# Block-sparse attention and a SwiGLU layer: scoring eight gathered key blocks per query block in place of all keys under a mask

## The chip, the cores and the metric

The kernel runs on one NeuronCore of a Trainium2 chip. Its five engines take their instructions in order, each from its own stream, and meet through semaphores: TensorE (PE; its weight loads are listed as PEld) multiplies matrices into PSUM, VectorE (DVE) and ScalarE (ACT) work elementwise, GpSimd (POOL) does small work and issues DMAs, SyncE (SP) issues DMAs. The metric is the device time of one execution in microseconds; lower is better.

## What is computed

Attention over 4 batches, 8 heads, 768 positions of 64 elements, followed by a gated layer over the 3072 tokens of 512 elements. Positions come in 24 blocks of 32. A query block attends its own block and the two neighbours, the first and the last block, and three blocks drawn for it in `sampled_blocks`; the first and the last query block attend everything.

```python
mask = np.abs(blk_i - blk_j) <= window
mask = mask | (blk_i == 0) | (blk_j == 0) | (blk_i == n_blocks - 1) | (blk_j == n_blocks - 1)
for qb in range(n_blocks):
    for kb in sampled_blocks[qb]:
        mask[qb * block:(qb + 1) * block, kb * block:(kb + 1) * block] = True
scores = np.where(mask, scores, -1000000000.0)
attn = softmax(scores);  out = attn @ v
...
xn = x / rms * rms_g
out = (silu(xn @ w_gate) * (xn @ w_val)) @ w_out      # 512 -> 1536 -> 512
```

## The kernel before

**Tiling.** Tokens go in groups: three of 256 tokens for batch 0, then two of 384 for each other batch. Within a group the heads follow one another. For one head, `scores` (L321 to L335) multiplies all 768 keys, six tiles of 128 on the output's partitions, with the group's queries as columns (L330), and one exponential on ScalarE takes 768 columns out of PSUM (L333). `values` (L337 to L343) multiplies each 128x128 piece of the exponentials, as the stationary operand, with the head's 64 value columns and two columns of ones (66 columns, L341); the ones column gives the sum, whose reciprocal (L350) scales the output into `stage` (L351).

**The mask** is part of the product: `KT` and `QT` carry, below their 64 rows of data, 24 rows that hold the key's block and the query's mask (88 rows in all). What is not attended is computed and comes out of the exponential as zero.

**The gated layer.** For a finished group, squares are summed on VectorE (L375), POOL takes the power -0.5 (L383), and x is scaled and turned, either by TensorE (L424, L428) or by a DMA transpose from SP (L395, L400). The FFN is cut into pieces (`ffn_pieces`): `gate(f)` (four matmuls, L442, then tanh on ScalarE, L446), `val(f)` (four matmuls, L453, then two VectorE instructions, L457 and L459) and `down` (L470, three matmuls a piece; the last one is copied out by ScalarE, L476, and stored by SP). Pieces share three PSUM buffers.

**What sets the order.** Every stream is written out by hand. The pieces of one group's FFN are spread at an even rate over the next group's heads: `position()` is called between the parts of the scores and emits what is due. The value products of a head come one head late (`late_pv`), and a group's FFN is entered two heads into the next group (`TX = 2`). The first group runs by itself (`first_group`), with matmuls on zeros (`keep_busy`) in TensorE's gaps. The last group's FFN forms the tail.

**Loads.** POOL loads K and Q with a cast to bf16 (L89, L81), V in float32 (L101) and the weights (L111, L553). VectorE casts V (L120). Batch 0's K and Q are turned by TensorE (L287) and copied by VectorE (L292). For later batches SP issues DMA transposes (L300) and further DMAs that put the halves in place (L308).

Of the kernel before, what the change touches and what calls it, by code (L numbers as in the profile page):

```python
# [11 lines left out]
I32 = mybir.dt.int32  # L12
# [6 lines left out]
def kernel(  # L19
# [20 lines left out]
    NB = S // 32  # L40
    NC = S // P
    DM = H * D
    DFF = moe_w_gate.shape[1]
    KD = DM // P
    MASKV = -65536.0
    SCALE = 1.0 / (D ** 0.5)
    NRND = sampled_blocks.shape[1]
    NF = DFF // P
    HC = NC // 2
    TGM = HC * P  # L50

    groups = [(0, c, 2) for c in range(0, NC, 2)]
    groups += [(b, c, HC) for b in range(1, B) for c in range(0, NC, HC)]
    FIRST = NC // 2
    KR = D + NB
    NP = H // 2
    VW = D + 2
    VS = D + 16
# [6 lines left out]
    work = ctx.enter_context(tc.tile_pool(name="work", bufs=1))  # L65
    ps_f = ctx.enter_context(tc.tile_pool(name="ps_f", bufs=3, space=bass.MemoryType.PSUM))
# [3 lines left out]


    qbf, kbf, vraw, qrest = {}, {}, {}, {}

    def load_q0(pr, lo, hi):

        if lo == 0:
            t = qbf[(0, pr)] = ld.tile([P, 2, 2 * D], BF16, name="q0", tag="q0", bufs=3)
        else:
            t = ld.tile([P, 2, NC * D], BF16, name="qbf", tag="qbf", bufs=4)[:, :, lo * D:]
            qrest[(0, pr)] = t  # L80
        nc.gpsimd.dma_start(  # L81
            out=t, in_=q[0, 2 * pr:2 * pr + 2].rearrange(
                "e (p c) d -> p e (c d)", p=P)[:, :, lo * D:hi * D])

    def load_one(b, pr, store, t=None):
        src, name = (k, "kbf") if store is kbf else (q, "qbf")
        if t is None:
            t = ld.tile([P, 2, NC * D], BF16, name=name, tag=name, bufs=4)
        nc.gpsimd.dma_start(  # L89
            out=t,  # L90
            in_=src[b, 2 * pr:2 * pr + 2].rearrange("e (p c) d -> p e (c d)", p=P))
        store[(b, pr)] = t

    def load_qk(b, pr):
        load_one(b, pr, kbf)
        load_one(b, pr, qbf)

    def load_v(b, pr):
        t = ld.tile([P, 2, NC, D], FP32, name="vraw", tag="vraw" if b else "vraw0",
                    bufs=2 if b else 4)  # L100
        nc.gpsimd.dma_start(  # L101
            out=t, in_=v[b, 2 * pr:2 * pr + 2].rearrange("e (p c) d -> p e c d", p=P))
        vraw[(b, pr)] = t
# [81 lines left out]
    for pr in range(1, NP):  # L185
        load_one(0, pr, kbf)
        load_q0(pr, 0, 2)
        if pr > 1:
            load_v(0, pr - 2)
# [641 lines left out]
```

## Time and profile before

| | |
|---|---|
| median of 3 runs | 309.54 us (309.23 to 316.04) |
| profiled execution | 309.93 us, its span 308.2 us |
| first FFN matmul | 26.23 us after the span's start |
| exponentials on ScalarE | 192, 813 ns each (768 columns) |
| score matmuls | 432: 288 of 384 columns, 144 of 256 |
| value matmuls | 1152 of 66 columns (a few are missing from the trace) |
| gate and value matmuls of the FFN | 432 each: 288 of 384 columns, 144 of 256 |
| POOL busy | 54.7 us, mostly the issue of DMAs at about 720 ns |
| DMA engines, share of the first 15 of 40 slices | 0.7 to 0.9 and over |

Lines of the profile read as: line of the kernel, engine, operation, output and inputs by the program's names with partitions x elements and type, count; busy time and mean of one in ns; idle time of the engine just ahead of it and what ended that. A matmul's duration holds its latency, so a run of matmuls takes less than the sum of its durations; the pace is read from runs of different lengths. Busy time of POOL counts the issue of its DMAs.

### The profile page before, as it was taken

The numbers are of one execution on the slowest core, as the hardware profiler recorded it, in microseconds if no ns is written. First come the engines' busy times: TensorE is split into PE (matmuls) and PEld (weight loads), VectorE is DVE, ScalarE is ACT, GpSimd is POOL, SyncE is SP. The second block draws the span as 40 slices with busy tenths as digits, with TensorE's granted clock in tenths as the row PEclk, the third lists the DMA queues.
The fourth block names the chain that finished last, engine by engine and source line by source line (L and its number), as shares of the span: only waits on it lengthen the run. The fifth ranks groups of instructions, "written<-read, shape, count | busy, mean of one in ns | idle before, by whom it ended". The sixth has DMA issues, their size and how long they took to land.

```text
span 308.2 us, 7249 instructions
## 1 busy us (share of the span) xinstructions
PE 299.9 (97%) x2843; PEld 198.9 (65%) x2863; DVE 203.6 (66%) x561; ACT 204.8 (66%) x330; POOL 54.7 (18%) x81
## 2 busy tenths in 40 slices
PE   8889999999999999999999999999999999999995
PEld 6676886985787566656666566655666566655653
DVE  7788884885578567763768457682767546675860
ACT  4886775776888677757776676676767667732331
POOL 9846201042220212012200122010000100010000
PEclk9999999999999999999999999999999999999999
DMA  7999999999999478526673379614000130002002
GB/s 124 276 210 201 208 215 151 171 173 245 218 205 146 112 154 162 109 48 189 113 156 85 81 176 148 140 25 139 16 2 0 42 115 2 0 5 100 2 0 103
DMA packets 61082, 36.71 MB, mean 119 GB/s; under 512 B 38348, under 2 KB 56640, under 8 KB 61048
## 3 DMA queue, kind: packets, MB, share of 16 engines
q0 software_dynamic: 17120, 17.90, 32.7%
q1 hardware_dynamic: 43892, 18.35, 27.5%
q8 instruction: 22, 0.36, 0.5%
q14 instruction: 12, 0.10, 0.1%
q10 hardware_dynamic: 36, 0.01, 0.0%
HBM read 28.59 MB, written 6.29 MB: 113 GB/s over the span
## 4 chain that ended last, share of the span: by engine, by line
PE 91%; POOL 3%; DMA 3%; DVE 2%; issue 1%; ACT 0%; POOLq 0%
PE gp L442 21%; PE vp L453 20%; PE yp L470 20%; PE st L330 18%; PE op L341 11%; DMA qbf<-in_q_dram 3%; POOL kbf L89 1%; PE tx L424 1%; POOL vraw L101 1%; POOL q L81 1%; DVE junk L375 1%; DVE stage L368 0%; PE tqk L287 0%; DVE xs L403 0%; POOL ki_i L183 0%
## 5 line engine op out<-in xcount | busy, mean ns | idle before, releaser
L333 ACT ACTIVATE ex<-st 128x768 bf16<-128x768 f32 x186 | 150.0, 813 | 53.7 <-PE st L330 51.9
L330 PE MATMUL st<-QT,KT 88*128 88x384 bf16 (+1 forms) x432 | 93.9, 309 | 1.4 <-DVE QT L292 1.0
L442 PE MATMUL gp<-xg,wg 128*128 128x384 bf16 (+1 forms) x432 | 80.8, 307 | 0.0
L453 PE MATMUL vp<-xg,wv 128*128 128x384 bf16 (+1 forms) x432 | 80.2, 307 | 0.0
L457 DVE SCALAR_TENSOR_TENSOR u<-th,gp 128x384 bf16<-128x384 bf16 (+1 forms) x108 | 54.8, 508 | 38.1 <-ACT th L446 36.6
L470 PE MATMUL yp<-wo,hps 128*128 128x512 bf16 (+1 forms) x283 | 71.9, 369 | 0.9
L446 ACT ACTIVATE th<-gp 128x384 bf16<-128x384 f32 (+1 forms) x108 | 49.1, 454 | 27.8 <-PE gp L442 27.5
L459 DVE TENSOR_TENSOR hps<-u,vp 128x384 bf16<-128x384 bf16 (+1 forms) x108 | 55.1, 510 | 11.3
L330 PEld LDWEIGHTS <-KT 88*128 88x128 bf16 x432 | 41.5, 98 | 26.1 <-DVE QT L292 2.0
L453 PEld LDWEIGHTS <-wv 128*128 128x128 bf16 x432 | 40.6, 97 | 20.6 <-issue 0.2
L442 PEld LDWEIGHTS <-wg 128*128 128x128 bf16 x432 | 40.1, 97 | 20.5 <-issue 0.3
L341 PEld LDWEIGHTS <-ex 128*128 128x128 bf16 x1116 | 42.8, 97 | 8.4 <-issue 0.2
L341 PE MATMUL op<-Vp,ex 128*128 128x66 bf16 x1116 | 44.9, 193 | 0.0
L470 PEld LDWEIGHTS <-hps 128*128 128x128 bf16 x300 | 27.6, 97 | 22.6 <-DMA wo<-in_moe_w_out_dram 0.3
L383 POOL TENSOR_TENSOR rstd<-ssq,mhalf 128x3 f32<-128x3 f32 (+1 forms) x9 | 7.4, 817 | 143.1 <-DVE ssq L375 143.1
L350 DVE RECIPROCAL rz<-op 128x3 f32<-128x3 f32 (+1 forms) x64 | 11.2, 174 | 24.0 <-PE op L341 23.7
L476 ACT ACTIVATE yo<-yp 128x512 f32<-128x512 f32 (+1 forms) x25 | 14.4, 577 | 15.4 <-PE yp L470 15.4
L351 DVE TENSOR_TENSOR stage<-op,rz 128x192 bf16<-128x192 f32 (+1 forms) x64 | 21.8, 341 | 2.2
L101 POOL DMA_DIRECT2D vraw<-in_v_dram x16 | 11.8, 739 | 59.3 <-DVE Vp L120 55.7
L375 DVE CUSTOM_DVE_ANT_0 junk<-stage 128x448 bf16<-128x448 bf16 (+1 forms) x24 | 14.7, 611 | 0.5
L395 DVE SCALAR_TENSOR_TENSOR xs<-stage,rstd,gain 128x512 bf16<-128x512 bf16 x15 | 10.4, 746 | 4.4 <-POOL rstd L383 4.4
L89 POOL DMA_DIRECT2D qbf<-in_q_dram x12 | 8.6, 721 | 16.8 <-DMA turned<-qbf 15.4
(71 smaller groups left out, 112.2 us busy)
## 6 DMA issues: line engine op xcount, KB each, us to landing
vraw<-in_v_dram POOLq DMA_DIRECT2D x16, 384.0 KB, 5.2
out_dram<-yo SPq DMA_DIRECT2D x23, 256.0 KB, 2.3
kbf<-in_k_dram POOLq DMA_DIRECT2D x15, 192.0 KB, 6.0
qbf<-in_q_dram POOLq DMA_DIRECT2D x12, 192.0 KB, 6.3
KT<-turned SPq DMA_DIRECT2D x24, 96.0 KB, 3.7
QT<-turned SPq DMA_DIRECT2D x22, 96.0 KB, 2.9
wg<-in_moe_w_gate_dram POOLq DMA_DIRECT2D x4, 384.0 KB, 10.7
wv<-in_moe_w_val_dram POOLq DMA_DIRECT2D x4, 384.0 KB, 12.1
```

Of the source, the lines that this page charges most:

```text
L101: nc.gpsimd.dma_start(out=t, in_=v[b, 2 * pr:2 * pr + 2].rearrange("e (p c) d -> p e c d", p=P))
L330: nc.tensor.matmul(out=at[:, e, 0:tg], lhsT=KT[b % 2][0:KR, h, jt * P:(jt + 1) * P], rhs=QT[b % 2][0:KR, h, c0 * P:c0 * P + tg], start=Tru ...
L333: nc.scalar.activation(out=ex[:, nj * part:nj * (part + 1), :], in_=at[:, 0:nj, 0:tg], func=AF.Exp, scale=SCALE)
L341: nc.tensor.matmul(out=op[:, it, 0:VW], lhsT=ex[:, jt, it * P:(it + 1) * P], rhs=Vp[b % 2][:, h, 2 * (jt % HC) + jt // HC, 0:VW], start=(j ...
L351: nc.vector.tensor_tensor(out=stage[:, 0:n, h * D:(h + 1) * D], in0=op[:, 0:n, 0:D], in1=rz[:, 0:n].unsqueeze(2).to_broadcast([P, n, D]), ...
L375: nc.vector.tensor_tensor_reduce(out=junk[:, 0:hi - lo], in0=part, in1=part, scale=1.0, scalar=(e["ssq"][:, it:it + 1] if lo else DM * 1e- ...
L442: nc.tensor.matmul(out=gp[:, 0:tg], lhsT=wg[:, c, f * P:(f + 1) * P], rhs=xg[:, c, 0:tg], start=(c == 0), stop=(c == KD - 1))
L446: nc.scalar.activation(out=th[:, 0:tg], in_=gp[:, 0:tg], func=AF.Tanh, scale=0.5)
L453: nc.tensor.matmul(out=vp[:, 0:tg], lhsT=wv[:, c, f * P:(f + 1) * P], rhs=xg[:, c, 0:tg], start=(c == 0), stop=(c == KD - 1))
L457: nc.vector.scalar_tensor_tensor(out=u[:, 0:tg], in0=th[:, 0:tg], scalar=1.0, in1=gp[:, 0:tg], op0=ALU.add, op1=ALU.mult)
L459: nc.vector.tensor_tensor(out=hps[:, f, 0:tg], in0=u[:, 0:tg], in1=vp[:, 0:tg], op=ALU.mult)
L470: nc.tensor.matmul(out=yp, lhsT=hps[:, f, tt * P:(tt + 1) * P], rhs=wo[:, f, lo:hi], start=(f == 0), stop=(f == NF - 1))
```

## The change

The whole attention part is rewritten. Work goes in 24 chunks of 128 queries (four query blocks of 32), six per batch: five with consecutive inner blocks, and one "edge" chunk with blocks 0, 23, 1 and 22. The edge chunk is the last of its batch, in the last batch the last but one. FFN groups are of 2, 2, 4, 4, 4, 4 and 4 chunks.

For each inner query block eight key blocks, 256 keys, are gathered: a window of three (three slots), three sampled ones and the two outer ones. `KT` and `QN` keep a head's even positions on 64 partitions and the odd ones on the other 64, so 256 keys are 128 columns of `kg`; the queries are laid out block-diagonally in `Qd`. One matmul of 64 columns per head and query block gives all its scores. Blocks 0 and 23 of the edge chunk are scored against all of `KT`. An exponential now takes 1024 columns.

Which sampled block a slot takes is computed on the chip at the start: 39 small VectorE instructions make a table of row indices `vidx`, and registers (44 on ScalarE, 22 on POOL) are loaded with offsets into `KT`. The window and outer keys are copied by VectorE, the sampled ones by ScalarE (two of three) and POOL, at addresses from the registers. Values are cast into `Vs` (batch 0 by ScalarE and VectorE, later ones by POOL) and written by SP to a DRAM table, one row of 2112 bytes for two positions and all heads. POOL gathers 128 rows of it per query block by an indirect DMA, 88 in all. Where a sampled block repeats one that is already there, its index points to rows of zeros, ones column included.

A value matmul has 32 columns of weights (one query block) and writes 32 partitions of PSUM, the four query blocks of a chunk in turn, so that the array is used in column tiles.

```diff
+    sizes = [2, 2, 4, 4, 4, 4, 4]
...
+    vtab = [dram.tile([NT + HB, 2 * HV], BF16, name=f"vtab{i}") for i in range(B)]
...
+    for eng, of in ((ET.Activation, range(NRND - 1)), (ET.Pool, range(NRND - 1, NRND))):
+        for r in of:
+            _, vals = nc.values_load_multi_w_load_instructions(
+                kofs[0:1, r * NB + 1:(r + 1) * NB - 1], engines=[eng], min_val=0, max_val=NT - HB,
...
+    def table(b):
+        nc.sync.dma_start(out=vtab[b][0:NT, :].rearrange("(p c) x -> p (c x)", c=HC),
+                          in_=Vs[b % 2].rearrange("p c h x -> p (c h x)"))
+
+    def turn(b, pr, which, copy, spare=False):
+        src = raw.pop((b, pr, which))
+        p_, tag = (ps_f, "ff") if spare else (ps_o, "ot")
+        t = p_.tile([P, 2, HC, P], BF16, name="tqk", tag=tag)
+        for e in range(2):
+            for cc in range(HC):
+                nc.tensor.transpose(out=t[:, e, cc, :], in_=src[:, e, cc * P:(cc + 1) * P],
+                                    identity=ident)
...
+    def gather_k(i, copy):
+        b, qbs = chunks[i]
+        kg = kgs[i] = work.tile([P, H, QB, P], BF16, name="kg", tag="kg", bufs=2)
...
+        copy(out=kg[:, :, j0:j0 + n, 0:WIN],
+             in_=spaced(src[:, :, (qbs[j0] - 1) * HB:(qbs[j0] - 1) * HB + WIN], step, n, WIN))
+        for w, at in ((0, 0), (1, NT - HB)):
+            copy(out=kg[:, :, j0:j0 + n, G0 + w * HB:G0 + (w + 1) * HB],
+                 in_=src[:, :, at:at + HB].unsqueeze(2).to_broadcast([P, H, n, HB]))
+
+    def sampled_k(i):
...
+            copy = act if r + 1 < NRND else pool
+            copy(out=kgs[i][:, :, j, R0 + r * HB:R0 + (r + 1) * HB],
+                in_=KT[b % 2][:, :, bass.ds(kat[(qbs[j], r)], HB)])
...
+    def gather_q(i, copy):
...
+            for a in range(2):
+                for w in range(2):
+                    src = QN[b % 2][w * D:(w + 1) * D, :, qbs[lo] * HB:(qbs[lo] + 1) * HB]
+                    copy(out=dst[a * D:(a + 1) * D, :, lo:hi, a, w, :],
+                         in_=spaced(src, step, hi - lo, HB))
+
+    def gather_v(i):
+        b, qbs = chunks[i]
+        vg = vgs[i] = work.tile([P, QB, 2 * HV], BF16, name="vg", tag="vg", bufs=2)
+        for j in range(QB):
+            if qbs[j] not in (0, NB - 1):
+                nc.gpsimd.indirect_dma_start(
+                    vg[:, j, :], None, vtab[b][:],
+                    bass.IndirectOffsetOnAxis(ap=vidx[:, qbs[j]:qbs[j] + 1], axis=0))
...
+            for j in range(2 if wide else 0, QB):
+                nc.tensor.matmul(out=st[:, at:at + UN], lhsT=kgs[i][:, h, j, :],
+                                 rhs=Qd[i % 2][:, h, j, :], start=True, stop=True)
...
+        def mm(hh, j, lhsT, rhs, n, of):
+            nc.tensor.matmul(out=op[j * BLK:(j + 1) * BLK, hh, :], lhsT=lhsT, rhs=rhs,
+                             start=(n == 0), stop=(n == of - 1))
...
+        if not in_order(i):
+            nc.vector.scalar_tensor_tensor(
+                out=xs, in0=stages[i], scalar=rstds[i], in1=gain, op0=ALU.mult, op1=ALU.mult)
+            nc.sync.dma_start_transpose(out=xg[:, :, at:at + P], in_=xs)
+            return
...
+    for i in range(len(chunks)):
...
+        scores(i, 0)
+        loads(i)
+        at(0)
+        if i > 0:
+            x_turned(i - 1)
+            if group_of[i - 1] != group_of[i]:
+                enter(group_of[i - 1], NPOS * len(groups[group_of[i]])
+                      + (4 if group_of[i] == len(groups) - 1 else 0))
+        scores(i, 1)
+        at(1)
...
+        if nx is not None and not newbatch and i > 0:
+            gather_v(nx)
+        at(2)
...
+        if nx is not None and not newbatch and i > 0:
+            gather_k(nx, dve)
+            gather_q(nx, dve)
+            dyn += sampled_k(nx)
+        at(3)
+        values(i, 0)
+        at(4)
+        at(5)
+        values(i, 1)
+        squares(i)
+        rms_power(i)
+        at(6)
+        at(7)
+        if nx is not None and (newbatch or i == 0):
+            if i == 0:
+                for pr in range(NP):
+                    turn(0, pr, 1, (act, dve)[pr % 2], spare=pr % 2)
+            gather_k(nx, dve)
+            gather_q(nx, dve)
+            for x in sampled_k(nx):
+                x()
+            gather_v(nx)
```

`at(n)` emits a chunk's side jobs (casts, turns and the table of the next batch), its share of the sampled copies for the next chunk, and the FFN pieces that are due; `NPOS` is 8 positions per chunk. `loads(i)` issues the next batch's V from SP and its K and Q from POOL. Tokens of chunks 0 to 3 and of the last group are turned by TensorE (four transposes and four scaled copies per chunk), the others by DMA transpose; stores go by query block, for the latter as two half-blocks each.

## The prediction

> **What bounds the kernel now.** I read the busy table first, then the chain that ended last, then the stretches by stage, and last single instructions in order of time.
>
> ```profile
> PE 299.9 (97%) x2843; PEld 198.9 (65%) x2863; DVE 203.6 (66%) x561; ACT 204.8 (66%) x330; POOL 54.7 (18%) x81
> ...
> PE 91%; POOL 3%; DMA 3%; DVE 2%; issue 1%; ACT 0%; POOLq 0%
> PE gp L442 21%; PE vp L453 20%; PE yp L470 20%; PE st L330 18%; PE op L341 11%; DMA qbf<-in_q_dram 3%; POOL kbf L89 1%; PE tx L424 1%; POOL vraw L101 1%; POOL q L81 1%; DVE junk L375 1%; DVE stage L368 0%; PE tqk L287 0%; DVE xs L403 0%; POOL ki_i L183 0%
> ```
>
> TensorE is busy for 97% of the span and carries 91% of the chain. The three FFN products are 61% of it, the scores 18%, the value products 11%. VectorE and ScalarE idle a third of the time, so a saving on them is worth nothing here; one on TensorE is worth its own length.
>
> The start matters too. In the next answer each line gives start, duration, engine, line and operation; the first is the first FFN matmul, the others give the pace of small value matmuls.
>
> ```profile
> 26.23 1.04 PE L442 MATMUL gp<-xg,wg 128*128 128x256 bf16 x4
> ...
> 14.43 0.89 PE L341 MATMUL op<-Vp,ex 128*128 128x66 bf16 x24
> 18.15 0.53 PE L341 MATMUL op<-Vp,ex 128*128 128x66 bf16 x12
> ```
>
> The FFN begins at 26.2 us; from there TensorE never rests. Twelve more value matmuls take 0.36 us more, so one with 66 columns costs 0.0303 us. In the same way (longer run minus single, or the chain's 4.53 us for 21) I get 0.058 us at 128 columns, 0.109 at 256, 0.1625 at 384, 0.216 at 512. With these paces the 282 us behind 26.2 come out as FFN 187 + scores 57 + values 32 + transposes 3 = 279, so the paces can be trusted.
>
> **The change, on TensorE after the FFN begins.** The FFN keeps its columns: 192 gate and value matmuls at 0.109, 480 at 0.216, 288 down matmuls at 0.216: 187 us. Scores: an ordinary chunk has 32 matmuls of 64 columns, about 0.0295 each (the 66-column row scaled): 0.94 us; an edge chunk 24 of 128 and 16 of 64: 1.86 us. Two chunks run before the FFN, so 18 x 0.94 + 4 x 1.86 = 24.5 us, against 57. Here the change gains 33 us.
>
> Value products: 64 matmuls of 66 columns per ordinary chunk, 128 per edge chunk; each now fills 32 output partitions. 18 x 64 + 4 x 128 = 1664 matmuls, against 1056. No row shows column tiles. If four run wholly side by side they cost 12.6 us, if one after another at the present pace 50.4. The nearest row is the present 66-column matmul, and nothing in the trace shows two matmuls overlapping beyond its pace; I take 50.4, 18 us more than now. K and Q of batches 1 to 3 are no longer turned by DMA but by 144 transposes at 0.058: 8.4 us; the x transposes add 1.5. Sum: 187 + 24.5 + 50.4 + 8.4 + 1.5 = 272 us, against 282 now. So TensorE gains 10 us at most by rows.
>
> **The start.** It becomes a longer chain. SP loads V and POOL loads K (0.72 us each to issue; POOL loads landed 7.2 us after issue in the first 30 us): all in at 11 us. VectorE first does 39 index instructions of about 0.17 us (the 24x24 mask rows took 0.15 to 0.24) behind the identity, until 12. Two casts each on VectorE (0.57) and ScalarE (0.81): 13.6. SP writes the 811 KB table to DRAM: at the 205 GB/s of the first 30 us 4 us, and 1.3 to issue: 19. Only then can POOL issue four gathers, at no less than a plain POOL load's 0.72: 22; landing 5 to 7 later: 28. Values of chunk 0 end at 30. The rest of Q is queued on POOL behind those gathers and lands at 32; its four turns (two deep on ScalarE and VectorE, 0.9 each) end at 34, the copies for chunk 1 at 36, its exponentials (1.03 each by the slope 490 to 813) at 38.5, its values at 41. Reciprocal 0.18, stage 0.42, squares 0.77, power 0.73, xs 0.40, transposes, four scaled copies at 0.34: 4 us. The FFN begins at **45 us**, 19 later. The 44 register loads on ScalarE and 22 on POOL, which stand ahead of the casts and gathers, appear in no row: between nothing and the 0.4 us of SP's shortest DMA issue, 17 us; I take them near nothing. So the start lies between 38 (loads landing at the whole run's median of 5 to 6) and 62.
>
> **What is exposed later.** At each of three batch borders the copies for the next chunk come behind the last FFN piece: VectorE needs one copy of 1536 elements and six of 512. SBUF copies of 512 and 768 elements took 292 and 345 ns here, so these are 0.55 and 0.28 us: 2.25 us; ScalarE's eight sampled copies take 0.255 each at least (its smallest row). The next scores wait some 4 us, three times: 12. Elsewhere these copies lie under FFN pieces; where VectorE is held up it costs their 2.25 us per chunk, 50 in all. Then the group entries: the FFN of chunks 8, 12, 16, 20 starts right behind x_turned of the chunk before. Its way is reciprocal to power 2.2, xs 0.75, DMA transpose landing after 2.4: 5.3 us and more, while TensorE has two positions and one score part, 2.8. I take 3 us each, 12. The old kernel waits two heads before it enters a group, so this exposure is new. The tail, 5 us of last scaling and store, is like the old one.
>
> Sum: 45 + 272 + 12 + 12 + 5 = 346 us of span. The profiled execution took 309.93 us for a span of 308.2, 1.7 more, and lies 0.4 above the median 309.54. So **348 us**.
>
> **Cover.** ScalarE sheds most: 56 exponentials of 1.03 us for 150 us, but gains 176 sampled copies (45 us or more). VectorE per chunk of a four-chunk group: three FFN pairs of 1.37, copies 2.25, normalisation 1.2, squares 0.77, xs 0.75 = 9.1 us against TensorE's 12. It is covered, with little to spare: at one element a cycle (1.05 ns each, the slope between its 256- and 384-column PSUM rows) the copies cost 5.8 and the sum 12.7. POOL has per chunk 3.7 gathers, as many small copies, power 0.8, loads 1, cast 0.7 (VectorE's took 0.55; POOL has no copy row): 6 us if a gather costs 0.72, 8.2 at its longest load issue, 1.29. SP issues eight stores per chunk at 0.4 to 0.8 us, under TensorE's 12. The DMA engines get 88 gathers of 264 KB, 24 MB more; a batch then moves some 12 MB in 75 us, 160 GB/s, where 200 were held early on.
>
> **Where POOL and VectorE meet.** Two lines of the timeline warn of a conflict between them:
>
> ```profile
> 1.64 0.83 POOL L183 IOTA ki_i<- 24x768 int32 x1
> 1.82 0.74 DVE L225 CAST ident<-ident 128x128 bf16<-128x128 f32 x1
> ```
>
> A cast of 128 elements took 0.74 us and ended just behind POOL's instruction, while casts of 768 take 0.55. The Trainium skill ("SBUF — State Buffer", Who interferes with whom) states that the two share a port pair that is locked for a whole instruction; the row agrees. By it each copy could wait half a POOL instruction, some 2.5 us per chunk, and VectorE would come to 11.6 of TensorE's 12.
>
> **Rivals.** (a) Column tiles overlap. The values then cost 12.6 instead of 50.4: 348 - 38 = 310, and with the start at 38 and half of the later exposures, 291. For it: the four outputs are disjoint partitions, issued in turn. Against: each has its own weight load. It decides from 11 ns per matmul on; then the result is no longer slower. The Trainium skill ("TensorEngine Tiling (Array Packing)", Key Properties) says that tiles load and multiply in parallel; by that page this rival would be the outcome, and no row here shows it. (b) Each switch between full and tiled work drains the array. 22 chunks have two halves with a switch in and out: 88 x 0.193 us, the latency of one value matmul, is 17 us: 365. The same section of the Trainium skill's page says that a mode change drains the array; no row shows that either. (c) POOL becomes the bound: with a gather at 3 us, 3.7 x 3 + 3.4 = 14.4 us per chunk, 45 + 22 x 14.4 + 31 (last group's FFN) + 5 + 2 = 400; at 2.5 us 359. It decides from about 2.3 us per gather. For it: nothing shows an indirect gather, and the lock row; against: plain issues are 0.72. I price it at 385. (d) That the change does not cut the work: it cuts score columns to 40%, but instruction counts rise from 432 + 1152 to 800 + 1792; this is inside the forecast.
>
> **Chances.** Forecast without drain 0.45 (332 to 360); (b) 0.15; (c) 0.20; (a) 0.20, its half with a short start below 303. Two per cent, about what a measurement of this kernel can tell from no change, is 303 to 316. Faster 0.10, within 0.10, slower 0.80. The 80% range leaves out the lower half of (a) and the upper half of (c): 303 to 385.
>
> **What would show it.** First FFN matmul at 45 us; 0.03 us or less per value matmul; gaps of TensorE of 3 to 4 us at batch borders and group entries; POOL instructions for gathers near 1 us; VectorE under 85%. I am wrong if value matmuls run below 15 ns, if the gathers take over 2 us, or if ScalarE's register-addressed copies cost far over 0.3 us: at 0.8 they would fill 141 us and delay the exponentials.

## The result

The changed kernel took 464.5 us (463.6 to 468.6), the kernel before, beside it, 310.1. The ratio is 1.502, 95% interval 1.490 to 1.514: slower by half, and 80 us above the upper end of the predicted range. Only the direction was right.

The page of the changed kernel, in the same two parts that the prediction showed of before, with a row between them: busy time with share of the span and instructions, then the granted clock in 40 slices (tenths of full speed), then the chain that ended last.

```profile
PE 312.5 (68%) x3786; PEld 175.6 (38%) x3833; DVE 236.7 (51%) x606; ACT 172.4 (37%) x372; POOL 173.9 (38%) x266
...
PEclk8755579979768798988688889878988979999999
...
issue 47%; POOL 24%; PE 19%; DVE 5%; ACT 2%; ACTq 1%; DMA 1%; POOLq 1%; DVEq 0%
POOL vg L329 16%; PE yp L471 6%; PE gp L443 5%; POOL kg L306 5%; PE vp L454 4%; PE st L352 2%; ACTq L234 1%; POOL kbf L104 1%; PE op L365 1%; DVE Qd L321 1%; POOL qbf L104 1%; PE tqk L267 1%; ACT ex L356 1%; POOL rstd L403 1%; DVE u L458 1%
```

The clock row of the kernel before, for comparison:

```profile
PEclk9999999999999999999999999999999999999999
```

No engine is full. TensorE, 97% busy before, is busy for 68%; the clock row, a 9 throughout where TensorE never rests, is a ragged 6 to 9 behind the start; and the chain is carried by "issue" (time in which the engine waited for nothing that the profile shows) and GpSimd, not by TensorE. The span in three stretches, cut at the first FFN matmul (58.1 us) and at the FFN of the last group (427 us), with busy time of each engine, granted clock, DMA share and GB/s:

```profile
0.00:58.10 58.10, 24.06 (x324) 16.63 (x326) 27.61 (x96) 15.78 (x36) 32.58 (x55) 0.63 0.86 188
58.10:427.00 368.90, 256.66 (x3311) 143.51 (x3352) 192.61 (x488) 146.24 (x319) 141.29 (x212) 0.87 0.49 112
427.00:462.10 35.10, 31.77 (x157) 15.48 (x158) 16.45 (x25) 10.34 (x18) 0.00 (x0) 1.00 0.18 50
```

With these the difference from the forecast of 346 us of span can be placed:

| term | forecast | measured | difference |
|---|---|---|---|
| start, to the first FFN matmul | 45 | 58.1 | +13 |
| TensorE busy behind it | 272 | 256.7 + 31.8 = 288.4 | +16 |
| TensorE idle behind it, with the end | 24 + 5 | 112.2 + 3.3 = 115.5 | +87 |
| span | 346 | 462.1 | +116 |

The idle time is the failed term. (47 of the 3833 matmuls are missing from this trace; by the trace of run 6, which has all of them, they are some 3 us of work.) What TensorE waited for over the whole span, from the list of the waits of its matmuls (waiting tile, releaser: us in total, times, longest):

```profile
PE gp L443 <- DMA xg<-xs: 29.6, 4, 9.8
PE tqk L267 <- DVE stage L388: 27.8, 12, 4.4
PE st L352 <- POOL kg L306: 19.5, 21, 2.4
PE st L352 <- DVE Qd L321: 15.8, 5, 5.2
PE op L365 <- DMA vg<-vtab,vidx: 9.9, 7, 2.7
PE vp L454 <- DVE u L458: 9.2, 7, 1.8
```

Between the first FFN matmul and the last group the six are 29.6, 27.0, 17.1, 7.4, 1.8 and 9.2 us; the rest of them lies in the start. That is five tiles and six releasers, most of them one to three microseconds at a time: not one late engine, but, as the experiments will show, queues that are in the wrong order at many places. The second entry is a turn of the next batch's keys or queries (`tqk`) that waits for the one PSUM buffer that it shares with the value sums. The third entry, once on TensorE and once on GpSimd (start, duration; in brackets the idle time before and what ended it):

```profile
164.68 1.03 PE L454 MATMUL vp<-xg,wv 128*128 128x512 bf16 x4
165.64 0.43 PE L365 MATMUL op<-vg,ex 128*32 128x66 bf16 x32
166.00 1.04 PE L443 MATMUL gp<-xg,wg 128*128 128x512 bf16 x4
...
167.73 0.22 PE L352 MATMUL st<-Qd,kg 128*128 128x64 bf16 x2
169.24 0.79 PE L352 MATMUL st<-Qd,kg 128*128 128x64 bf16 x14 [1.29 <-POOL kg L306]
```

```profile
168.36 0.58 POOL L403 TENSOR_TENSOR rstd<-ssq,mhalf 128x1 f32<-128x1 f32 x1 [12.43 <-DVE ssq L397]
168.91 0.52 POOL L306 COPY kg<-KT 128x128 bf16 x2
```

GpSimd had been idle for 12.4 us. The last two sampled copies for the next chunk were issued behind the power of the present chunk, which waits for its squares, which wait for its value sums. So the scores of a chunk wait for the normalisation of the one before, by the order of issue alone. SyncE's queue does the same at a group entry:

```profile
291.98 9.21 SPq L493 DMA_DIRECT2D out_dram<-yo  x16
301.28 1.20 SPq L420 DMA_TRANSPOSE xg<-xs  x1
```

```profile
303.75 1.89 PE L443 MATMUL gp<-xg,wg 128*128 128x512 bf16 x4 [6.46 <-DMA xg<-xs]
```

Sixteen stores stand ahead of the transpose that the next group's FFN needs: some 7 us of issue, and 2 us of waiting for ScalarE's next scaled output, which ended at 297.5 us. The transpose's own input, `xs`, had been ready since 294.8. The queue is not all of it. At the entries of 155.2 and 229.9 us the transpose was issued 5.3 and 6.0 us ahead of the FFN's first matmul, with the DMA engines full in that time (share 1.10 and 1.18); at the other two it was 2.5 us, with the share below 0.5. The last line of the two views shows the second price too: four gate matmuls take 1.89 us behind that gap and 1.04 in the lines above, where TensorE had not rested.

### The profile page after: what moved, and what is told of

Its sections match the earlier page's. It is cut to its first block, busy times and chain, and to the rows that moved or that the text cites. A ratio compares the mean times of both kernels' runs of the same rounds, so it can differ in the third digit from the quotient of the medians.

```text
span 462.1 us, 9859 instructions
## 1 busy us (share of the span) xinstructions
PE 312.5 (68%) x3786; PEld 175.6 (38%) x3833; DVE 236.7 (51%) x606; ACT 172.4 (37%) x372; POOL 173.9 (38%) x266
## 4 chain that ended last, share of the span: by engine, by line
issue 47%; POOL 24%; PE 19%; DVE 5%; ACT 2%; ACTq 1%; DMA 1%; POOLq 1%; DVEq 0%
POOL vg L329 16%; PE yp L471 6%; PE gp L443 5%; POOL kg L306 5%; PE vp L454 4%; PE st L352 2%; ACTq L234 1%; POOL kbf L104 1%; PE op L365 1%; DVE Qd L321 1%; POOL qbf L104 1%; PE tqk L267 1%; ACT ex L356 1%; POOL rstd L403 1%; DVE u L458 1%
## 5 line engine op out<-in xcount | busy, mean ns | idle before, releaser
L443 PE MATMUL gp<-xg,wg 128*128 128x512 bf16 (+1 forms) x325 | 86.3, 387 | 30.2 <-DMA xg<-xs 29.6
L329 POOL DMA_INDIRECT vg<-vtab,vidx x88 | 89.0, 1012 | 26.4 <-issue 25.1
L458 DVE SCALAR_TENSOR_TENSOR u<-th,gp 128x512 bf16<-128x512 bf16 (+1 forms) x84 | 51.1, 608 | 92.3 <-ACT th L447 90.8
L454 PE MATMUL vp<-xg,wv 128*128 128x512 bf16 (+1 forms) x320 | 86.6, 391 | 11.0 <-DVE u L458 9.2
L356 ACT ACTIVATE ex<-st 128x1024 bf16<-128x1024 f32 x56 | 57.5, 1026 | 86.0 <-PE st L352 68.0
L447 ACT ACTIVATE th<-gp 128x512 bf16<-128x512 f32 (+1 forms) x84 | 45.1, 537 | 94.3 <-PE gp L443 85.3
L352 PE MATMUL st<-Qd,kg 128*128 128x64 bf16 x704 | 43.7, 206 | 35.8 <-POOL kg L306 19.5
L461 DVE TENSOR_TENSOR hps<-u,vp 128x512 bf16<-128x512 bf16 (+1 forms) x84 | 51.4, 612 | 28.9 <-PE vp L454 20.8
L352 PEld LDWEIGHTS <-kg 128*128 128x128 bf16 x704 | 35.7, 106 | 47.5 <-POOL kg L306 34.5
L454 PEld LDWEIGHTS <-wv 128*128 128x128 bf16 x336 | 34.8, 109 | 41.5 <-issue 19.6
L306 ACT COPY kg<-KT 128x128 bf16 x176 | 40.8, 300 | 0.0
L267 PE MATMUL tqk<-ident,qbf 128*128 128x128 bf16 x96 | 10.2, 262 | 29.6 <-DVE stage L388 26.2
```

Source lines behind the costliest of these rows:

```text
L306: copy(out=kgs[i][:, :, j, R0 + r * HB:R0 + (r + 1) * HB], in_=KT[b % 2][:, :, bass.ds(kat[(qbs[j], r)], HB)])
L329: nc.gpsimd.indirect_dma_start(vg[:, j, :], None, vtab[b][:], bass.IndirectOffsetOnAxis(ap=vidx[:, qbs[j]:qbs[j] + 1], axis=0))
L352: nc.tensor.matmul(out=st[:, at:at + UN], lhsT=kgs[i][:, h, j, :], rhs=Qd[i % 2][:, h, j, :], start=True, stop=True)
L356: nc.scalar.activation(out=ex, in_=st, func=AF.Exp, scale=SCALE)
L443: nc.tensor.matmul(out=gp[:, 0:tg], lhsT=wg[:, c, f * P:(f + 1) * P], rhs=xg[:, c, 0:tg], start=(c == 0), stop=(c == KD - 1))
L447: nc.scalar.activation(out=th[:, 0:tg], in_=gp[:, 0:tg], func=AF.Tanh, scale=0.5)
```

## The experiments

Theory: the loss is in waits that come from the order of the in-order queues, with the clock falling in the gaps. Rivals: an engine's load (GpSimd, VectorE, or TensorE at its granted clock), switches of TensorE between tiled and whole form, the transfers.

**1. Sampled copies ahead of the power.**

```diff
-            for _ in range(-(-len(dyn) // max(1, NPOS - n))):
+            for _ in range(-(-len(dyn) // max(1, 6 - n))):
```

> One edit of the changed kernel: all twelve sampled-key copies of the next chunk are issued before the current chunk's normalisation power, so that no sampled copy stands behind it on GpSimd. Theory (the loss is in the order of the in-order queues): TensorE's wait on the GpSimd copies of kg, 43.5 us in 44 waits, falls below 15 us, and the time by 15 to 40 us, to 425 to 450 us. Rival (GpSimd is bound by its gathers and copies): its work is unchanged, so the time stays within 2% of 464.5 us, and the same wait is only named otherwise. Rival (switches of TensorE between its tiled and whole forms): nothing changes, 464 us.

455.4 us, ratio 1.473 (1.461 to 1.484). The wait for GpSimd's copies is gone from the list, all of it, but only 9 us came back: the theory's range was missed, and the time is just within the rival's 2%. What stands there now:

```profile
PE gp L443 <- DMA xg<-xs: 37.1, 4, 14.9
PE tqk L267 <- DVE stage L388: 22.9, 10, 5.4
PE st L352 <- DVE Qd L321: 16.4, 5, 5.6
PE tqk L267 <- DMA vg<-vtab,vidx: 12.2, 3, 4.2
```

The wait for xg grew by 7.5 us, and that of a turn for the gathers from 2.6 to 12.2. "Named otherwise" is what the rival had foreseen, though not for its reason: GpSimd is as idle as before (busy for 38% in both).

**2. Every chunk turned by TensorE**, so that no transpose stands in SyncE's queue.

```diff
     def in_order(i):
-        return i < 4 or i in groups[-1]
+        return True
```

> One edit of the changed kernel: every chunk is normalised and turned by TensorE with the four-token-run layout of its first four chunks, so the DMA transposes on SyncE's queue go, a chunk's output takes four or fewer stores for eight, and TensorE gets four transposes and VectorE four scaled copies more a chunk for 16 chunks. Theory (the transposes stand on SyncE behind output stores that wait for ScalarE): the wait of the first gate matmul for xg (29.6 us at four entries) goes, against 64 transposes of some 0.1 us and their eviction: 10 to 30 us less, 435 to 455 us. Rival (SyncE's queue hides, the entries would wait for something else): 460 to 470 us. Rival (VectorE is what is late): the 64 scaled copies at some 0.3 us add, 470 to 485 us.

450.8 us, ratio 1.460 (1.453 to 1.467): 14 us, inside the expectation. The 29.6 us for xg went; waits for VectorE's xs (14.8 us, before 2.9) and of the value sums for their buffer (12.0, before 2.9) came.

**3. Registers split.** Only the first chunk's blocks are loaded ahead of the work, the rest inside the first chunk.

```diff
-                kofs[0:1, r * NB + 1:(r + 1) * NB - 1], engines=[eng], min_val=0, max_val=NT - HB,
+                    kofs[0:1, r * NB + lo:r * NB + hi], engines=[eng], min_val=0,
...
+    registers(2, 6)
...
         scores(i, 1)
         at(1)
+        if i == 0:
+            registers(6, NB - 1)
+            registers(1, 2)
```

> One edit of the changed kernel: only the four blocks of the first chunk are loaded to registers ahead of the first work (4 for 22 in each of three loads); the rest are loaded in the first chunk. Theory (ScalarE stands 9.7 us in two loads of 22 registers ahead of its value casts, at some 0.22 us a register): two loads of 4 take about 2 us, the casts start some 7 us sooner, the first FFN matmul comes at 50 to 53 us for 58.1, and the time falls by 5 to 9 us, to 455 to 460 us. Rival (the loads' time is fixed per load, or the start waits for the DMA of the keys): the first FFN matmul stays at 57 to 59 us and the time within 2 us of 464.

The first FFN matmul moved from 58.1 to 53.8 us, a little later than the expected 50 to 53. The time, 461.5 us, ratio 1.490 (1.481 to 1.500), can't be told from the changed kernel's. The loads had cost what their rows say, in the changed kernel (duration in ns, min, median, max):

```profile
L234 ACTq TENSOR_LOAD <-kofs x2: 4753/4838/4922, 8.4 to 13.3; - x2
L234 POOLq TENSOR_LOAD <-kofs x1: 5171/5171/5171, 13.2 to 13.2; - x1
```

Each loads 22 registers: 0.22 us a register on ScalarE, 9.7 us in a row ahead of its casts of V. With four registers a load took 1.0 us.

**4. VectorE's key and query copies behind the first value sums.**

```diff
-        if nx is not None and not newbatch and i > 0:
-            gather_k(nx, dve)
-            gather_q(nx, dve)
-            dyn += sampled_k(nx)
-        at(3)
         values(i, 0)
+        if nx is not None and not newbatch and i > 0:
+            gather_k(nx, dve)
+            gather_q(nx, dve)
+            dyn += sampled_k(nx)
+        at(3)
```

> One edit of the changed kernel: VectorE's copies of the next chunk's keys and queries are issued behind the reciprocal and product that empty the one PSUM buffer of the value sums, and not ahead of them. Theory (order on VectorE): TensorE's wait on that buffer, 27 us in 11 waits, falls below 10 us, but the key copies and the sampled copies behind them come later by some 1.5 us in each chunk; the time falls by 5 to 20 us, to 445 to 460 us. Rival (the gathered keys are the later of the two): the waits of the scores on kg grow by what the buffer gives, 460 to 475 us.

459.0 us, ratio 1.478 (1.469 to 1.486): 5.5 us, inside the expectation, though not its wait. The wait for the buffer halved (27.8 to 13.7 us, where below 10 was expected), that for VectorE's u grew (9.2 to 14.7), that for the gathers too (9.9 to 13.4).

**5. The four together.** Its diff is the sum of the four.

> The four edits of the first four experiments together (early sampled copies, every chunk turned by TensorE, registers split, key and query copies behind the first value sums). They gave 9, 14, 3 and 5.5 us alone. Theory (waits in the order of the queues, each hiding the next, with the granted clock falling in the gaps): together they give more than their sum of 31 us, 395 to 430 us, with a granted clock above 0.90 in the middle. Rival (each edit only moves the wait to the next link of one chain through every chunk, so that they overlap): less than the sum, 435 to 450 us.

424.0 us, ratio 1.368 (1.359 to 1.378): 40.5 us, inside the theory's range; the rival's "less than the sum" is out. That it is more than the 31 of the four alone is not shown: the time of the changed kernel, known to some 4 us (95%), enters the difference of 9 us three times. From the first FFN matmul to the last group TensorE's idle time fell from 112 to 82 us and the clock there rose from 0.87 to 0.91.

**6. Value matmuls tile by tile.**

```diff
-                for w in range(2):
-                    for j in range(QB):
-                        mm(hh, j, ex[:, j, w, :], vg[:, j, w, h, :], w, 2)
...
+            for j in range(QB):
+                for hh in range(4):
...
+                    for w in range(2):
+                        mm(hh, j, ex[:, j, w, :], vg[:, j, w, half * 4 + hh, :], w, 2)
```

> One edit of the changed kernel: the 32 value matmuls of a half chunk run column tile by column tile (eight in a row to the same 32 columns), and not in turn over the four. Theory (four tiles overlap because neighbours go to different columns): a run of 32 takes 0.9 to 1.2 us for 0.42, and the time rises by 5 to 30 us. Rival (the pace of 7 ns is that of the narrow weights, wherever they go): 0.40 to 0.45 us a run, time unchanged.

The same half chunk, first in the changed kernel and then here:

```profile
159.90 0.42 PE L365 MATMUL op<-vg,ex 128*32 128x66 bf16 x32
```

```profile
162.60 0.83 PE L365 MATMUL op<-vg,ex 128*32 128x66 bf16 x32
```

A single one takes 0.20 us, so the other 31 cost 7 ns each where neighbours go to different columns of the array, and 20 ns where eight in a row go to the same. The overlap is real and comes from the order. The value matmuls' busy time rose from 29.8 to 47.8 us, in 40 half chunks (the edge chunks are as before), and the kernel moved from 464.5 to 467.6 us in a single time, which is no more than its times differ among themselves: a run is a little shorter than the 0.9 to 1.2 us expected, and the 5 us of the kernel's time were not reached. That TensorE's own work hardly counts was the first hint of the next result.

**7. Less work on TensorE.**

```diff
-            for f in range(part * NF // NQ, (part + 1) * NF // NQ):
+            for f in range(part * NF // NQ, part * NF // NQ + 1):
...
```

> The changed kernel with two of every three matmuls of the down product left out (the output is then not the sum over all hidden columns): 192 matmuls of 512 columns less, 41.5 us of TensorE work at full clock. Theory (the time is that of a chain of waits through each chunk, and TensorE's load only fills it): the time falls by less than 20 us, to 445 to 464 us, and TensorE stands idle for the rest. Rival (TensorE's work at the clock that it is granted is the bound): 41.5 us or more go, 410 to 423 us.

445.3 us, ratio 1.440 (1.433 to 1.446): 19 us for 41.5 us of work taken away, at the upper edge of the theory's "less than 20". Up to its last group TensorE was idle 123 us (112), at a clock of 0.80 (0.87). TensorE's load is not the bound; more than half of what was taken away turned into waiting and a slower clock.

**8. More work on TensorE.**

```diff
+        keep_busy(4, 512)
         scores(i, 1)
...
+        keep_busy(4, 512)
         values(i, 0)
         at(4)
         at(5)
+        keep_busy(4, 512)
         values(i, 1)
```

> The changed kernel with four unread matmuls of 512 columns added at three places in each chunk (ahead of the second score group and of both value groups): 62 us more of TensorE work at full clock. Theory of the clock (half of the loss is the half clock that follows each gap): the granted clock in the middle rises from 0.87 to above 0.95, and the time stays within 15 us of 464 or falls. Theory of the waits alone: the unread matmuls fill gaps that are there anyway, but those that don't fit add; 470 to 495 us. Rival (TensorE's work is the bound): 520 to 530 us.

487.8 us, ratio 1.573 (1.564 to 1.583): 62 us of added work cost 23, as the theory of the waits alone said. The clock rose to 0.91 only, and filling the gaps did not pay for itself. TensorE's busy time over the span grew by 55.5 us (368.0 for 312.5), or some 52 with the missing matmuls counted, so the kernel's own matmuls took 7 to 10 us less. The clock is part of the loss, but what makes the gaps has to go, not the gaps.

**9. A chunk's sums one chunk behind its scores.** The loop is rewritten; its core, for chunk i:

```diff
+            values(i - 1, 0)
+            at(0)
+            sc(0)
+            at(1)
+            values(i - 1, 1)
+            squares(i - 1)
+            rms_power(i - 1)
+            gather_v(i)
...
+            x_scaled(i - 1)
+            at(4)
+            if nx is not None:
+                gather_k(nx, dve)
+                dyn.extend(sampled_k(nx))
+            at(5)
+            sc(3)
+            x_turned(i - 1)
```

> The changed kernel's computation, with each chunk's value sums and normalisation moved one chunk behind its scores: while chunk i is scored, chunk i-1 is summed, so that each chain (scores, exponentials, value sums, normalisation, turn; key copies, scores) has a whole chunk to run in. With it two PSUM buffers for the value sums and four for the FFN (the scores get two of one bank for two of two banks), every chunk turned by TensorE, registers split, the rest of the first batch's queries loaded ahead of the first gathers. TensorE's work is the same. Theory (a chain of waits through each chunk sets the time): TensorE's idle time in the middle falls from 112 us to below 40 and its clock rises above 0.95, 315 to 360 us. Rival (an engine's load or the gathers' transfers set it, whatever the order): 400 us or more, with one engine other than TensorE above 85% busy in the middle. Rival (each edit only moves the wait to the next link): 380 to 420 us.

412.4 us, ratio 1.331 (1.322 to 1.341): by the time alone the rival of the moved wait, and TensorE was idle for 73 us in the middle where the theory had below 40. But the list of waits is another one. Every entry but one is below 8 us now:

```profile
PE op L369 <- DMA vg<-vtab,vidx: 63.1, 54, 4.3
```

The rewritten loop issues the gathers of a chunk behind the power of the chunk before, in the chunk just ahead of the sums that read them. GpSimd issues the four at 0.95 us and 0.30 between, and in the answer on transfers each lands 3.8 us after its issue (median of 88). I had ordered around every wait but this one.

**10. Gathers a whole chunk ahead.**

```diff
-            gather_v(i)
+            if nx is not None and nx != PB:
+                gather_v(nx)
```

and the start reordered, as the expectation says. The next chunk's key copies move too, to the head of the loop, which the expectation does not say.

> The lagged kernel with two changes. The value gathers are issued a whole chunk ahead of the chunk whose sums read them (in the lagged run they stood on GpSimd behind the power of the chunk before, were issued at 0.96 us each and landed 3.8 us after their issue, and TensorE waited 63 us for them in 54 waits). And the start: the remaining registers are loaded four blocks at a time, a chunk ahead of their use; the second gather stands directly behind the first; the next batch's value loads wait behind them on GpSimd's queue; the first two chunks' sums run before the FFN's first matmul. Theory (the landing of the gathers is what was late, and nothing else of their cost matters): the wait for vg falls below 15 us, the first FFN matmul comes at 42 to 46 us for 52.4, and the time falls by 50 to 75 us, to 335 to 360 us. Rival (the gathers are bound by their rate, 88 of them sharing queues with the loads): they land as late as before, 395 to 412 us. Rival (VectorE, 9.8 us a chunk, takes over as the bound): 360 to 385 us, with VectorE above 85% in the middle.

351.6 us, ratio 1.138 (1.131 to 1.146): 61 us from order alone, as the theory said. The wait for the gathers falls from 63.1 to 14.2 us, 6.3 of it at one batch border; the first FFN matmul comes at 49.9, later than expected. From it to the last group, in the ninth run and here:

```profile
52.40:376.60 324.20, 251.54 (x3361) 145.83 (x3404) 203.10 (x545) 145.69 (x363) 135.22 (x209) 0.88 0.46 119
```

```profile
49.90:314.50 264.60, 228.85 (x3389) 136.02 (x3434) 200.58 (x546) 149.24 (x367) 137.53 (x212) 0.95 0.58 150
```

Nearly the same instructions and busy time on VectorE, ScalarE and GpSimd. TensorE's idle time goes from 73 to 36 us, and its busy time from 252 to 229 as the clock rises from 0.88 to 0.95. VectorE, at 76% of this stretch, is not the bound.

**11. Start and border.** The next batch's first gather in its turn, powers ahead of the loads on GpSimd.

```diff
-            if nx is not None and nx != PB:
-                gather_v(nx)
-            if i == PB:
-                gather_v(i)
+            if nx is not None:
+                gather_v(nx)
...
```

> The kernel of the run before with its two largest remaining gaps taken out. At the border of the first batch the gather of the next batch's first chunk was issued behind that of its second, and TensorE stood 6.3 us and then 3 more at 107 to 116 us; it is issued in its turn now. At the start the normalisation powers stood on GpSimd behind six to ten DMA issues of 0.75 us; these now follow them, and the second chunk is scored ahead of the first value sums. Theory (waits in queue order): the first FFN matmul comes at 41 to 45 us for 49.9, the gap at the border goes, and 12 to 22 us fall, to 330 to 340 us. Rival (VectorE, 84% busy in the middle, or the transfers of the weights, 231 GB/s at 45 to 100 us, are late next): 342 to 350 us.

348.4 us, ratio 1.128 (1.123 to 1.133). Both repairs worked: the first FFN matmul comes at 43.9 us, the wait for the gathers is 0.6 us. But only 3 us are left of it, at the edge of the noise and in the rival's range, since the new order on GpSimd made a new wait, on TensorE:

```profile
54.57 0.22 PE L356 MATMUL st<-Qd,kg 128*128 128x64 bf16 x2
68.70 0.69 PE L356 MATMUL st<-Qd,kg 128*128 128x64 bf16 x6 [13.91 <-POOL kg L310]
```

and, on GpSimd, what stood ahead of the two copies that it waited for:

```profile
58.17 0.95 POOL L333 DMA_INDIRECT vg<-vtab,vidx  x1 [0.30 <-issue]
62.37 0.89 POOL L595 DMA_DIRECT2D wo<-in_moe_w_out_dram  x1 [3.26 <-DMA wo<-in_moe_w_out_dram]
...
67.35 0.75 POOL L104 DMA_DIRECT2D qbf<-in_q_dram  x1
68.36 0.52 POOL L310 COPY kg<-KT 128x128 bf16 x2 [0.27 <-issue]
```

The load of the output weights was not issued for 3.3 us, until an earlier one had landed, and everything behind it on GpSimd stood as well. That it waited for room in the queue is likely, but not shown: in the changed kernel, too, a load of `wg` waited 3.9 us on GpSimd for a load of K, with which it shares no tile. I had missed that an issue can block.

**12 and 13. Copies ahead of the loads, then the loads spread.**

```diff
+            while dyn and i < 4:
+                dyn.pop(0)()
...
-        return [lambda j=j, r=r: one(j, r) for j in range(QB) if qbs[j] not in (0, NB - 1)
-                for r in range(NRND)]
+        return [lambda j=j, r=r: one(j, r) for r in reversed(range(NRND)) for j in range(QB)
+                if qbs[j] not in (0, NB - 1)]
...
-            pairs = {3: [0, 1], 4: [2, 3]}.get(s, ())
+            pairs = {3: [(1, 0)], 4: [(0, 1), (1, 2)], 5: [(0, 3)]}.get(s, ())
```

The first two parts are of run 12, the third is of run 13, which moves the loads in the same way. Run 13 also issues the key copies and the gathers for the second batch's first chunk later in the chunk before it, which its expectation does not say; run 14 keeps that.

> The kernel of the run before with GpSimd's sampled copies of the next chunk issued ahead of its value gathers, and in the first chunks ahead of the loads of the output weights and of the next batch, which are spread over two chunks. In the run before TensorE stood 13.9 us at 54.8 us for two such copies behind four gathers and seven loads, one of which waited 3.3 us for room in its queue, and 26.6 us in ten waits of this kind in all. Theory (waits in queue order to the last): the wait for GpSimd's copies falls below 6 us and the time by 16 to 26 us, to 322 to 332 us. Rival (the transfers, 233 GB/s at 45 to 100 us, are the bound there, and the loads are then late): the gain at 45 to 100 us is less than half, 335 to 345 us.

> The kernel of the run before with the next batch's loads and turns spread: two pairs of heads loaded in the third chunk, one in the fourth, one in the fifth, turned half a chunk to a chunk later than they were, and the second half of the output weights loaded in the fourth chunk for the third. In the run before, TensorE stood 13.4 us at 61 us for keys of the next batch whose load had been issued behind the weights. Theory (queue and transfer order in the first 100 us): that wait goes and none of its size takes its place, 322 to 338 us. Rival (the bytes themselves are the bound from 45 to 100 us, some 11 MB at 210 to 235 GB/s): a wait for another tile of 8 us or more stands in its place, 342 to 355 us.

Both miss, theory and rival alike: 362.7 us, ratio 1.176 (1.169 to 1.182), and 356.7 us, 1.154 (1.150 to 1.158). In run 12 the wait for GpSimd's copies is gone and 13.4 us of waiting for the next batch's keys, now issued later, stand in its place.

**14. The order of the copies put back.**

> The kernel of the run before with the sampled copies issued block by block again, as in all runs up to the eleventh (the last two issued GpSimd's four first and ScalarE's eight behind them). In the run before TensorE made stops of about 0.5 us inside runs of scores and value matmuls, 14 us in all, with no releaser shown, against 2 us in the eleventh run. Theory A (these stops come from the order of the copies: the matmuls wait for ScalarE's last copies): they go, and the time falls by 12 to 22 us, to 335 to 345 us. Theory B (they come from TensorE's own stream of instructions, and the copies had long been done): they stay or come at other places, 350 to 358 us.

354.7 us, ratio 1.146 (1.142 to 1.150): theory B. The stops stay, with no releaser shown, and what they are remains open:

```profile
PE op L369 <- issue: 6.5, 13, 1.2
PE st L356 <- issue: 3.8, 5, 1.5
```

The stretch from 45 to 100 us is better here than in run 11, and still not good, though the first FFN matmul comes later (46.5 us for 43.9). That stretch in run 11 and in this one:

```profile
45.00:100.00 55.00, 36.68 (x586) 27.49 (x584) 32.04 (x97) 28.46 (x75) 36.88 (x54) 0.84 1.02 233
```

```profile
45.00:100.00 55.00, 42.75 (x581) 29.83 (x581) 33.37 (x102) 27.80 (x68) 41.20 (x55) 0.83 1.09 258
```

The DMA share is above 1 in both, and TensorE is still idle for 12 us, now with waits for keys (5.8 us the longest) and output weights (2.8). Weights, the next batch's inputs, table and gathers all have to move there, so order alone seems to have little more to give in this stretch; that is read from the share, and no run took bytes away.

## Why the prediction was wrong, and where it was right

**The step that failed is "What is exposed later".** It named three batch borders and four group entries, 24 us, and said that elsewhere the copies "lie under FFN pieces". (It priced a hold-up of VectorE there at 50 us, and left it out of the sum.) TensorE was idle for 112 us from the first FFN matmul to the last group. Of the named places, the entries took 29.6 us for 12. At all four the transpose stands, with its input ready, behind stores that SyncE issues in order (2.8, 7.3, 6.5 and 7.2 us): the cover step had compared the stores' issue time with TensorE's 12 us and not asked what they wait for, nor what stands behind them. At the first two the transpose itself also took 5.3 and 6.0 us from its issue to the FFN's first matmul, beside full DMA engines, where 2.4 was forecast. The borders took less than forecast in the wait that they were priced by (VectorE's copies to Qd, 7.4 us in three waits for 12). The others were not in the forecast's sum at all: the single buffer for the value sums behind VectorE's copies (27.0 us), GpSimd's copies behind the power (17.1), VectorE's u (9.2), the gathers' landing (4.4 us, with the 2.6 of a turn that waited for them). Run 1 removes the wait for GpSimd's copies, run 2 that of the entries and run 4 about half of that for the buffer, each by the place or the kind of a few instructions. In runs 1 and 2 less than half of the removed wait comes back as time, and other waits grow. Runs 9 and 10 show that the same sums, on the same engines and with more PSUM buffers, take 352 us in another order. So the cover by sums (9.1 of 12 us per chunk on VectorE, 6 to 8 on GpSimd) was right, since the two were busy for 8.8 and 6.4 us per chunk, and said nothing about the order.

**TensorE's work.** The paces were good (sixteen score matmuls at 171.60 us are followed by the next instruction at 172.06, 0.029 us each) except for the value products: 26.2 us busy in the stretch where 50.4 were forecast. Rival (a) had the mechanism. The Trainium skill ("TensorEngine Tiling (Array Packing)", Key Properties) has tiles load and multiply in parallel; the 7 ns of the changed kernel agree. The 20 ns of run 6 add that neighbours have to differ in their tile. I had set the row (30 ns) above the page where the row was of another kind of matmul. By that rival the result would have been 291 to 310: the 24 us that it gave were there, and were lost in the idle time.

**The clock was not in the forecast.** Less the 24 us, the forecast's work up to the last group (272 less the last group's 31) is 217 us; TensorE was busy 257. Of the 40 us between, the mean granted clock of 0.87 makes some 32 (217 / 0.87 = 249), by this estimate; the other 8 may be the latency of single matmuls, and no run separates them. In the rows shown, four gate matmuls run at half pace behind the gap of 6.46 us. The Trainium skill ("TensorE: Matmul & The Clock Gate", HAM oscillation — how this bites in real kernels) says that gaps above some 3.4 us bring the array back to half rate. The row of 6.46 us agrees, but two others of the changed kernel do not fit a limit on the single gap:

```profile
251.71 0.80 PE L267 MATMUL tqk<-ident,qbf 128*128 128x128 bf16 x6 [2.53 <-DVE stage L388]
```

```profile
287.48 0.49 PE L267 MATMUL tqk<-ident,qbf 128*128 128x128 bf16 x6 [4.39 <-DVE stage L388]
288.02 3.29 PE L471 MATMUL yp<-wo,hps 128*128 128x512 bf16 x8
```

Behind 2.53 us six transposes run at half pace at once; behind 4.39 us they run at full pace, and only the eight down matmuls behind them at half (3.29 us, where six took 1.46 at 281.3); the granted clock was 1.00 up to 288.3 us and 0.50 from 288.4 to 291.7. So from one gap's length it can't be told here whether and when the clock falls. What it means for a forecast: idle time on a full engine can cost more than itself, here 112 us of idle and an estimated 32 of slower matmuls.

**The start** was 13 us late. The register loads, priced "near nothing" under an upper bound of 17, took 9.7 us on ScalarE and 5.2 on GpSimd; run 3 got 4.3 us of it back at the first FFN matmul. The rest is again order: the other queries of the first batch were loaded behind the gathers and turned only at 38 to 42 us. Reordered, with the registers four blocks at a time, the FFN starts at 43.9 us (run 11), about the forecast's 45.

**The rivals.** (b) The drain is smaller than 0.193 us: in the lines of the result the fourth vp matmul would be followed at 165.54 us by another, and the tiled run starts at 165.64; the gate matmuls start 0.13 us behind the run's last issue. That is some 0.2 us for a switch in and out, 44 times, about 10 us and not 17, an estimate from this one place. (c) The gathers took 0.96 us (median) and 0.30 between them, below the 2.3 from which it decides, and GpSimd was busy for 38%. What counted of the gathers, in run 9 above all, was not their cost but their landing, 3.8 us later. (d) did not come: the work was cut as said. The rival that came true, a chain of waits through each chunk, was not on the list; the lock between GpSimd and VectorE decided nothing, with VectorE at 52% of the stretch: its 120 copies of 512 elements took 0.32 and 0.34 us on the mean for a forecast of 0.28, some 6 us more in all, where the lock had been priced at 2.5 us per chunk.

**What the change is worth with most of its waits out.** 348.4 us in the best order found. That this is the number of the forecast is chance: the value products cost less than forecast, and the waits more. It is still 38 us above the kernel before. 17.7 us of these are the start (43.9 for 26.2). In run 11 TensorE is idle for 26 us between 45 and 150 us and for 11 from there to its last group, where the kernel before had 1 up to its last group; the smaller work, 262 us busy behind the first FFN matmul for 278, gives 16 of it back. A version that beats the kernel before was not found.

## What to carry to other kernels

When a full engine's work is cut, its cover goes with it: for every instruction that the change adds, ask what it waits for and what stands behind it in its queue, stores and DMA issues included, because sums of busy time per engine say only that an order without waits exists. Give each chain (scores, exponentials, sums, normalisation, turn) a whole iteration to run in, and count a gather by its landing, not by its issue. One repaired wait mostly shows the next one; four local repairs together gave 40 us here, a loop that gives every chain its iteration, with the gathers ahead, 113.

## What was not expected of the hardware

- Tiled value matmuls cost 7 ns each in turn over four column tiles and 20 ns eight in a row to one, against 30 ns for the whole-array form with the same 66 columns.
- A register load costs 0.22 us per register on ScalarE with 22 in one instruction, and 0.25 with four.
- A DMA issue on GpSimd can block its queue (3.3 us) until an earlier transfer has landed.
- The granted clock can fall behind a gap of 2.5 us of TensorE, and can hold through one of 4.4 us and fall 0.9 us later.
- Runs of small matmuls on TensorE sometimes stop for half a microsecond with no releaser shown: 1 us in run 11 and 10 us in run 14, among some 2,500 such matmuls. Its cause is open.
